# Decode attention with a gated MLP mix: K one pair ahead of V, and the weighted sum of V in four column groups

## The chip, the cores and the metric

The kernel runs on one core of a Trainium2 chip. The metric is the time of one execution on the device in microseconds (us); a kernel's figure is the median over repeated runs. A profile is taken of one further execution; its "span" reaches from the first to the last instruction.

## What is computed

Two branches get the same two rows `x` (batch B = 2, one position, D = 1024) and are mixed by a gate. Branch A is attention against a long cache: 32 heads, 16384 positions, 128 elements a head, all in bf16.

```python
# A: attention of one query row against the cache
q = (x @ wq) split in 32 heads                    # B, H, 1, 128
scores = einsum("bhqd,bhkd->bhqk", q, k_cache) * 128 ** -0.5
p = softmax(scores)
a = (einsum("bhqk,bhkd->bhqd", p, v_cache) as rows) @ wo
# B: a small MLP on the same rows
h = gelu(layernorm(x) @ w1); hs = shifted(h) @ w2; x1 = x + hs
b = x1 + gelu(layernorm(x1) @ w3) @ w4
# mix
g = sigmoid(sum(x * gate_w)); out = g * a + (1 - g) * b
```

With one position every shifted quarter of `h` is zero, so `hs` is zero. K and V of one batch row and head are 4 MB each; the 64 pairs (b, h) together are 537 MB. The weights add some 35 MB.

## The kernel before, in words

**Tiles.** A pair's K (and V) is one tile of 128 partitions; partition p holds 128 successive positions (index j) of 128 elements. All big transfers (K, V, halves of wq, blocks of B's weights) share one pool of five slots of that size (`big`, L60). Blocks of wo (256 KB, one a head) have a pool of three.

**A pair.** The loop at L487 goes over the 64 pairs, in order of heads, with both batch rows of a head one after the other. It calls, for pair i:

- `qk_stage` (L252): K lies with positions on partitions, but the scores need its elements there. VectorE transposes K in 32x32 blocks, in eight pieces (`T`, L260), each taken as 32-bit words. Four matmuls for each piece, with a sparse copy of q (`z`, built by GpSimd at L238) as the stationary operand and 512 columns of `T` as the moving one, add up all scores of the pair in one PSUM tile `S` of 128x512 (L268).
- `softmax_stage` (L276): VectorE takes the row maxima (`m`, L279), TensorE transposes them (L281), VectorE reduces them to one (`mx`, L283), TensorE spreads it over the partitions (L285), VectorE copies it out (`nb`, L287). ScalarE computes the exponentials and row sums (`Pr`, `rs`, L290), VectorE transposes the result in 32x32 blocks (`PT`, L294).
- `pv_stage` (L298): the total of the row sums by an fp32 matmul (L304) and its reciprocal (`rinv`, L306). Then the weighted sum of V, called PV below: for each of the 128 j a matmul with V[:, j, :] as the stationary operand and one column of PT as the moving one (L309), all into one column `oc`. VectorE scales it into `OT` (L316). After the second pair of a head two matmuls with the block of wo add to `wo_acc` (L322).

**Loads.** All big loads are issued by SyncE (SP) on one queue, written out by hand: at the end of pass i come V of i+2, a block of B's weights at six of the passes, a wo block at every second one, and K of i+3. Each waits until its slot is free. So the order on the queue is ..., V(i+2), K(i+3), V(i+3), K(i+4), .... The last V (pair 63) comes in four pieces of 64, 32, 16 and 16 of the j; the last wo block follows it. B's stages run two passes after their load.

**Order on the engines.** Every engine works through its own list in order. A scheduler orders the lists from the program, by priorities near its order.

Of the kernel before, what the change touches and what calls it, by code (L numbers as in the profile page):

```python
# [10 lines left out]
FP32 = mybir.dt.float32  # L11
# [12 lines left out]
def kernel(  # L24
# [15 lines left out]
    nc = tc.nc  # L40
# [30 lines left out]
    def misc_psum(shape, dtype):  # L71
        return mps.tile(shape, dtype, tag="misc", name="misc")
# [7 lines left out]
    def load_rows(src, r0, rn, name):  # L80

        N = src.shape[1]
        t = big_tile(name)
        nc.sync.dma_start(
            out=t[:, : rn * N].rearrange("p (r n) -> p r n", n=N),
            in_=src.rearrange("(p r) n -> p r n", p=P)[:, r0 : r0 + rn, :],
        )
        return t[:, : rn * N].rearrange("p (r n) -> p r n", n=N)

    kn_tiles = {}  # L90
    vn_tiles = {}
    V_SPLIT_LAST = [NJ // 2, NJ // 4, NJ // 8, NJ // 8]

    def issue_k(i):
        if i >= NPAIR:
            return
        b, h = pairs[i]
        t = big_tile("Kn")
        nc.sync.dma_start(
            out=t[:].rearrange("p (j d) -> p j d", d=Dh),  # L100
            in_=A_k_cache[b, h].rearrange("(p j) d -> p j d", p=P),
        )
        kn_tiles[i] = t

    def issue_v(i):
        if i >= NPAIR:
            return
        b, h = pairs[i]
        t = big_tile("Vn")
        tv = t[:].rearrange("p (j d) -> p j d", d=Dh)  # L110
        src = A_v_cache[b, h].rearrange("(p j) d -> p j d", p=P)
        j0 = 0
        for n in V_SPLIT_LAST if i == NPAIR - 1 else [NJ]:
            nc.sync.dma_start(out=tv[:, j0 : j0 + n, :], in_=src[:, j0 : j0 + n, :])
            j0 += n
        vn_tiles[i] = t

    wo_tiles = {}

    def load_wo(h):  # L120
        if h >= H:
            return
        t = wpool.tile([P, D], BF16, tag="woh", name="woh")
        nc.sync.dma_start(out=t[:], in_=A_wo[h * Dh : (h + 1) * Dh, :])
        wo_tiles[h] = t

    wq_half = [load_rows(A_wq, r * (KC // 2), KC // 2, f"wq{r}") for r in range(2)]

    x_pm = const.tile([P, B, KC], BF16)
    with nc.allow_non_contiguous_dma(reason="4 KB"):  # L130
# [3 lines left out]
    gw_row = rows.tile([B, D], BF16, tag="tmp_bf")  # L134
    for b in range(B):
        nc.scalar.dma_start(out=gw_row[b : b + 1, :], in_=gate_w.rearrange("(o d) -> o d", o=1))

    issue_k(0)
    issue_v(0)
    issue_k(1)  # L140


    ident_bf = const.tile([P, P], BF16)
# [24 lines left out]
    nc.vector.memset(own[:], 0.0)  # L168
    for a in range(4):
        nc.vector.memset(own[32 * a : 32 * a + 32, 4 * a : 4 * a + 4], 1.0)  # L170
    ZW = P + 8
    NZ = 3
    z_tiles = []
# [31 lines left out]
    def compute_q():  # L205
        q_f = const.tile([P, H, B], FP32)
        for half in range(2):
            qps = misc_psum([P, H, B], FP32)
            rn = KC // 2
            for h in range(H):  # L210
                for r in range(rn):
                    nc.tensor.matmul(  # L212
                        qps[:, h, :],
                        lhsT=wq_half[half][:, r, h * Dh : (h + 1) * Dh],
                        rhs=xT[:, half * rn + r, :],
                        start=(r == 0),
                        stop=(r == rn - 1),
                    )
            if half == 0:
                nc.vector.tensor_copy(out=q_f[:], in_=qps[:])  # L220
            else:
                nc.vector.tensor_tensor(out=qT[:], in0=q_f[:], in1=qps[:], op=ALU.add)
        qs_ps = misc_psum([P, 4, NPAIR], FP32)
        for v in range(4):
            nc.tensor.matmul(
                qs_ps[:, v],
                lhsT=selv[:, v].rearrange("p a w -> p (a w)"),
                rhs=qT[:].rearrange("p h b -> p (h b)"),
                start=True,
                stop=True,  # L230
            )
        nc.vector.tensor_copy(out=qsel[:], in_=qs_ps[:].rearrange("p v n -> p n v"))

    def build_z(i):
        if i >= NPAIR:
            return
        z = z_tiles[i % NZ]
        nc.gpsimd.tensor_tensor(  # L238
            out=z[:, :, 7 : 7 + P].rearrange("p v (x e) -> p v x e", e=8)[:, :, :, 0],
            in0=qsel[:, i, :].unsqueeze(2).to_broadcast([P, 4, 16]),  # L240
            in1=own[:].unsqueeze(1).to_broadcast([P, 4, 16]),
            op=ALU.mult,
        )
# [32 lines left out]
    def softmax_stage(i):  # L276
# [18 lines left out]
        PT_tiles[i] = PT  # L295
        rs_tiles[i] = rs

    def pv_stage(i):  # L298
        b, h = pairs[i]
        PT = PT_tiles.pop(i)  # L300
        rs = rs_tiles.pop(i)
        V = vn_tiles.pop(i)[:].rearrange("p (j d) -> p j d", d=Dh)
        tot_ps = misc_psum([P, 1], FP32)
        nc.tensor.matmul(tot_ps[:], lhsT=quarter_f[:], rhs=rs[:], start=True, stop=True)  # L304
        rinv = stat.tile([P, 1], FP32, name="rinv")
        nc.vector.reciprocal(out=rinv[:], in_=tot_ps[:])  # L306
        oc = ops.tile([P, 1], FP32, name="oc")
        for j in range(NJ):
            nc.tensor.matmul(  # L309
                oc[:],  # L310
                lhsT=V[:, j, :],
                rhs=PT[:, j % CJ, j // CJ : j // CJ + 1],
                start=(j == 0),
                stop=(j == NJ - 1),
            )
        nc.vector.tensor_scalar(  # L316
            out=OT[:, h, b : b + 1], in0=oc[:], scalar1=rinv[:, 0:1], scalar2=None, op0=ALU.mult
        )
        if b == B - 1:
            woh = wo_tiles.pop(h)  # L320
            for n in range(DH2):
                nc.tensor.matmul(  # L322
                    wo_acc[n][:],
                    lhsT=OT[:, h, :],
                    rhs=woh[:, n * W : (n + 1) * W],
                    start=(h == 0),
                    stop=(h == H - 1),
                )


    def layernorm_rows(src_row, dst_row_bf):
# [72 lines left out]
    h2_acc = const.tile([P, FC, B], FP32)  # L404
    h2T = const.tile([P, FC, B], BF16)
    wt = {}
    b_ps = []

    def linear_rows(w, actT, r0, rn, dst, first, last):
        for r in range(rn):  # L410
            for n in range(DH2):
                nc.tensor.matmul(  # L412
                    dst[n][:],
                    lhsT=actT[:, r0 + r, :],
                    rhs=w[:, r, n * W : (n + 1) * W],
                    start=(first and r == 0),
                    stop=(last and r == rn - 1),
                )

    def st_ln1():  # L420
        layernorm_rows(x_row[:], xn_row[:])
        rows_to_T(xn_row[:], xn1T[:])
# [23 lines left out]
    def st_lin3(half):  # L446
        linear_cols(wt.pop(f"w3{half}"), xn2T, half * (KC // 2), KC // 2, FC, h2_acc[:], half == 0)
        if half == 1:
            gelu_T(h2_acc[:], h2T[:], FC)

    def st_lin4(half):
        if half == 0:
            b_ps.extend(misc_psum([B, W], FP32) for _ in range(DH2))
        linear_rows(wt.pop(f"w4{half}"), h2T, half * (FC // 2), FC // 2, b_ps, half == 0, half == 1)
        if half == 1:
            for n in range(DH2):
                sl = slice(n * W, (n + 1) * W)
                nc.vector.tensor_tensor(out=pre_row[:, sl], in0=x1_row[:, sl], in1=b_ps[n][:], op=ALU.add)
            nc.vector.tensor_scalar(
                out=pre_row[:], in0=pre_row[:], scalar1=omg_row[:, 0:1], scalar2=None, op0=ALU.mult  # L460
            )

    def w_load(key, src, r0, rn):
        wt[key] = load_rows(src, r0, rn, "wt")


    extra = [
        (4, lambda: w_load("w1", B_w1, 0, KC), st_lin1),
        (8, lambda: w_load("w2", B_w2, 0, KC), st_lin2),
        (14, lambda: w_load("w30", B_w3, 0, KC // 2), lambda: st_lin3(0)),  # L470
        (20, lambda: w_load("w31", B_w3, KC // 2, KC // 2), lambda: st_lin3(1)),
        (28, lambda: w_load("w40", B_w4, 0, FC // 2), lambda: st_lin4(0)),
        (32, lambda: w_load("w41", B_w4, FC // 2, FC // 2), lambda: st_lin4(1)),
    ]
    ex_load = {s * NPAIR // 64: ld for s, ld, _ in extra}
    ex_run = {s * NPAIR // 64 + 2: fn for s, _, fn in extra}

    compute_q()
    compute_gate()
    load_wo(0)  # L480
    issue_v(1)
    issue_k(2)
    build_z(0)
    build_z(1)
    st_ln1()

    for i in range(NPAIR):  # L487
        build_z(i + 2)
        qk_stage(i)
        softmax_stage(i)  # L490
        pv_stage(i)
        if i in ex_run:
            ex_run[i]()
        issue_v(i + 2)
        if i in ex_load:
            ex_load[i]()
        if i % B == B - 1:
            load_wo((i + 1) // B)
        issue_k(i + 3)

    out_row = rows.tile([B, D], BF16, tag="tmp_bf")
    for n in range(DH2):
# [40 lines left out]
```

## Time and profile before

| | |
|---|---|
| time before, median of 10 runs | 1362.32 us (1361.96 to 1363.09) |
| profiled execution, time | 1363.06 us |
| profiled execution, span | 1361.1 us |
| read from HBM | 572.53 MB, 421 GB/s over the span |
| mean granted TensorE clock | 0.737 |
| instructions in the profile, all engines | 24487 |

The page has, from the top: busy time of each engine; 40 slices of the span with tenths of busy time, the granted clock of TensorE and the rate of the DMA engines; the DMA queues; the chain of work that ended last, followed back from the end; and the costliest groups of instructions with the idle time before them and what ended it. PE is TensorE's matmuls, PEld its weight loads, DVE VectorE, ACT ScalarE, POOL GpSimd, SP SyncE. "L260" is a line of the kernel. A group reads: line, engine, operation, written tile <- read tile, shapes, count, busy us, mean ns, idle us before it and its releaser. In a row of windows the first number is the length, then busy us and count of PE, PEld, DVE, ACT and POOL, then granted clock, DMA share and GB/s.

### The profile page before, as it was taken

How to read it: one execution, taken by the hardware profiler on the slowest of the kernel's cores; microseconds unless marked ns; L12 is line 12 of the kernel's file. 1: busy time of each engine (PE TensorE's matmuls, PEld its weight loads, DVE VectorE, ACT ScalarE, POOL GpSimd, SP SyncE). 2: the span in 40 equal slices, each digit the busy share in tenths (PEclk: the TensorE clock that was granted, in tenths of full speed). 3: DMA queues.
4: the chain of work that ended last, by engine and by line, in shares of the span. 5: the costliest groups of instructions: out<-in, count | busy, mean ns of one | idle time of the engine just before them, and what ended most of it. 6: DMA issues, size and time to landing. Idle time of an engine off the chain costs nothing.

```text
span 1361.1 us, 24487 instructions
## 1 busy us (share of the span) xinstructions
PE 974.6 (72%) x11196; PEld 530.1 (39%) x11260; DVE 749.0 (55%) x948; ACT 51.8 (4%) x132; POOL 33.9 (2%) x79
## 2 busy tenths in 40 slices
PE   2776777777767676777777777767767767776776
PEld 2333344344344344434434343333433334334343
DVE  2655555565636554565545456546645655654654
ACT  0000000000000000000000000000000000000000
POOL 0000000000000000000000000000000000000000
PEclk9877767687766786876777777677678667777767
DMA  9999999999999999999999999999999999999993
GB/s 401 435 423 433 433 425 430 429 429 430 428 431 429 428 429 431 430 428 429 430 429 432 427 427 432 429 429 429 427 432 430 430 427 431 430 430 428 430 424 158
DMA packets 25011, 574.11 MB, mean 422 GB/s; under 512 B 3014, under 2 KB 3014, under 8 KB 7372
## 3 DMA queue, kind: packets, MB, share of 16 engines
q1 hardware_dynamic: 24628, 572.54, 98.3%
q8 instruction: 88, 1.44, 0.4%
q14 instruction: 15, 0.12, 0.0%
q10 hardware_dynamic: 280, 0.01, 0.0%
HBM read 572.53 MB, written 0.00 MB: 421 GB/s over the span
## 4 chain that ended last, share of the span: by engine, by line
DMA 68%; PE 19%; DVE 9%; issue 3%; ACT 1%; DVEq 0%; POOL 0%; ACTq 0%
DMA Kn<-in_A_k_cache_dram 66%; PE S L268 12%; DVE T L260 6%; PE oc L309 5%; DMA x_pm<-in_A_x_dram 2%; ACT Pr L290 1%; DVE PT L294 1%; DVE m L279 1%; PE misc L285 1%; PE misc L212 1%; PE misc L412 0%; DVE mx L283 0%; PE misc L281 0%; DVE nb L287 0%; DVE x_row L437 0%
## 5 line engine op out<-in xcount | busy, mean ns | idle before, releaser
L268 PE MATMUL S<-T,z 128*128 128x512 bf16 x1984 | 595.6, 455 | 174.8 <-DVE T L260 158.7
L260 DVE STREAM_TRANSPOSE T<-Kn 128x1024 f32<-128x1024 f32 x512 | 596.3, 1217 | 132.6 <-DMA Kn<-in_A_k_cache_dram 106.7
L268 PEld LDWEIGHTS <-z 128*128 128x128 bf16 x2048 | 227.8, 111 | 544.4 <-issue 389.8
L309 PEld LDWEIGHTS <-Vn 128*128 128x128 bf16 x8192 | 233.0, 103 | 23.2 <-issue 23.2
L309 PE MATMUL oc<-PT,Vn 128*128 128x1 bf16 x8192 | 224.7, 165 | 18.9 <-DVE rinv L306 15.8
L316 DVE TENSOR_SCALAR OT<-oc,rinv 128x1 bf16<-128x1 f32 x64 | 14.1, 221 | 226.2 <-PE oc L309 226.2
L290 ACT ACTIVATE Pr<-S,nb 128x512 bf16<-128x512 f32 x64 | 44.0, 687 | 1247.9 <-DVE nb L287 1247.9
L279 DVE TENSOR_REDUCE m<-S 128x1 f32<-128x512 f32 x64 | 44.3, 692 | 74.7 <-PE S L268 74.7
L304 PE MATMUL misc<-rs,quarter_f 128*128 128x1 f32 x128 | 28.7, 293 | 71.6 <-ACT Pr L290 71.6
L294 DVE STREAM_TRANSPOSE PT<-Pr 128x512 bf16<-128x512 bf16 x64 | 45.5, 711 | 57.9 <-ACT Pr L290 57.9
L238 POOL TENSOR_TENSOR z<-qsel,own 128x64 bf16<-128x64 bf16 x64 | 30.2, 479 | 1216.1 <-PE S L268 1209.3
L304 PEld LDWEIGHTS misc<-rs,quarter_f 128*128 128x128 f32 x128 | 23.2, 227 | 77.1 <-ACT Pr L290 77.1
L281 PE MATMUL misc<-ident_f,m 128*1 128x128 f32 x64 | 17.3, 270 | 50.1 <-DVE m L279 50.1
L285 PE MATMUL misc<-mx,nscale_f 1*128 1x1 f32 x128 | 24.2, 256 | 23.7 <-DVE mx L283 23.7
L322 PE MATMUL wo_acc<-woh,OT 128*2 128x512 bf16 x64 | 32.4, 609 | 10.0 <-DVE OT L316 10.0
L281 PEld LDWEIGHTS misc<-ident_f,m 128*1 128x1 f32 x64 | 5.1, 79 | 83.0 <-DVE m L279 83.0
L285 PEld LDWEIGHTS misc<-mx,nscale_f 1*128 1x128 f32 x128 | 18.7, 182 | 35.9 <-DVE mx L283 35.9
L283 DVE TENSOR_REDUCE mx<-misc 1x1 f32<-1x128 f32 x64 | 17.8, 278 | 23.2 <-PE misc L281 23.2
L287 DVE COPY nb<-misc 128x1 f32<-128x1 f32 x64 | 10.1, 158 | 30.1 <-PE misc L285 30.1
L212 PE MATMUL misc<-xT,wq 128*128 128x2 bf16 x256 | 7.1, 165 | 25.8 <-DVE xT L180 23.2
L412 PE MATMUL misc<-wt,h2T 128*2 128x512 bf16 x56 | 18.2, 503 | 2.6 <-DMA wt<-in_B_w_dram 2.6
L385 PEld LDWEIGHTS <-wt 128*128 128x128 bf16 x288 | 18.4, 172 | 1.3 <-DMA wt<-in_B_w_dram 0.7
(60 smaller groups left out, 90.4 us busy)
## 6 DMA issues: line engine op xcount, KB each, us to landing
Kn<-in_A_k_cache_dram SPq DMA_DIRECT2D x64, 4096.0 KB, 41.5
Vn<-in_A_v_cache_dram SPq DMA_DIRECT2D x63, 4096.0 KB, 40.0
wt<-in_B_w_dram SPq DMA_DIRECT2D x4, 3584.0 KB
wq<-in_A_wq_dram SPq DMA_DIRECT2D x2, 4096.0 KB, 17.1
woh<-in_A_wo_dram SPq DMA_DIRECT2D x32, 256.0 KB, 39.9
wt<-in_B_w_dram SPq DMA_DIRECT2D x2, 2048.0 KB
Vn<-in_A_v_cache_dram SPq DMA_DIRECT2D x1, 2048.0 KB
Vn<-in_A_v_cache_dram SPq DMA_DIRECT2D x1, 1024.0 KB
```

Source lines behind the costliest of these rows:

```text
L212: nc.tensor.matmul(qps[:, h, :], lhsT=wq_half[half][:, r, h * Dh : (h + 1) * Dh], rhs=xT[:, half * rn + r, :], start=(r == 0), stop=(r == ...
L238: nc.gpsimd.tensor_tensor(out=z[:, :, 7 : 7 + P].rearrange("p v (x e) -> p v x e", e=8)[:, :, :, 0], in0=qsel[:, i, :].unsqueeze(2).to_bro ...
L260: nc.vector.transpose(out=T[:].rearrange("p w j s -> p j w s"), in_=Kw[:, m * CW : (m + 1) * CW].rearrange("p (j w e) -> p j w e", w=2, e=32),
L268: nc.tensor.matmul(S[:], lhsT=z[:, v, 7 - m : 7 - m + P], rhs=Tb[:, v // 2, :, v % 2], start=(m == 0 and v == 0), stop=(m == NM - 1 and v ...
L279: nc.vector.reduce_max(out=m[:], in_=S[:], axis=AX.X)
L281: nc.tensor.transpose(mT[:], m[:], ident_f[:])
L285: nc.tensor.matmul(nb_ps[:], lhsT=nscale_f[:], rhs=mx[:], start=True, stop=True)
L290: nc.scalar.activation(out=Pr[:], in_=S[:], func=ACTF.Exp, bias=nb[:], scale=scale, accum_out=rs[:])
L294: nc.vector.transpose(out=PT[:].rearrange("p j m -> p (j m)"), in_=Pr[:])
L304: nc.tensor.matmul(tot_ps[:], lhsT=quarter_f[:], rhs=rs[:], start=True, stop=True)
L309: nc.tensor.matmul(oc[:], lhsT=V[:, j, :], rhs=PT[:, j % CJ, j // CJ : j // CJ + 1], start=(j == 0), stop=(j == NJ - 1),)
L322: nc.tensor.matmul(wo_acc[n][:], lhsT=OT[:, h, :], rhs=woh[:, n * W : (n + 1) * W], start=(h == 0), stop=(h == H - 1),)
```

## The change

It does four things.

1. **Order.** Transfers and steps are two lists. The steps run as: scores of pair i+1, PV of pair i, wo, a stage of B, softmax of pair i+1. The transfers have the same order: K(i+1), a block of B's weights, a wo block, V(i). A transfer is issued as soon as the step that frees its slot stands in the program. The last transfers are K63, V62, V63 in four pieces, and the last wo block. The first five big ones are the halves of wq, K0, K1 and V0.
2. **PV.** For all pairs but the last, `pv_rows` has V as the moving operand. Eight rounds m; in each, four matmuls write 32 partitions each of one PSUM tile `O` (128x512): group g takes four of the j as 512 moving columns, and all four groups have the same 32 columns of PT as the stationary operand. ScalarE copies `O` out to `Os`, and four fp32 matmuls with a selection matrix `osel` pick the wanted rows and add them up into the column `oc`. The last pair keeps the form of before (`pv_cols`).
3. **wo** has a step of its own, and its load comes one pair earlier on the queue.
4. **B.** The last linear stage adds each half to the row at once instead of keeping two PSUM tiles over several passes; the blocks are loaded two passes later by number, and used in the same pass.

```diff
+    osel = const.tile([P, 4], FP32)
+    nc.vector.tensor_copy(out=osel[:], in_=ident_f[:, 0:8:2])
+    for g in range(1, 4):
+        nc.vector.tensor_tensor(
+            out=osel[:], in0=osel[:], in1=ident_f[:, 40 * g : 40 * g + 8 : 2], op=ALU.add
+        )
...
+    def pv_rows(V, PT, oc):
+        O = ops.tile([P, 4 * Dh], FP32, name="O")
+        for m in range(NM):
+            lhsT = PT[:].rearrange("p j m -> p (j m)")[:, m : CJ * 32 : 16]
+            for g in range(4):
+                j0 = m * CJ + 4 * g
+                nc.tensor.matmul(
+                    O[32 * g : 32 * g + 32, :],
+                    lhsT=lhsT,
+                    rhs=V[:, j0 : j0 + 4, :],
+                    start=(m == 0),
+                    stop=(m == NM - 1),
+                )
+        Os = rows.tile([P, 4, Dh], FP32, name="Os")
+        nc.scalar.copy(out=Os[:].rearrange("p x d -> p (x d)"), in_=O[:])
+        for x in range(4):
+            nc.tensor.matmul(
+                oc[:], lhsT=Os[:, x, :], rhs=osel[:, x : x + 1], start=(x == 0), stop=(x == 3)
+            )
...
-        oc = ops.tile([P, 1], FP32, name="oc")
-        for j in range(NJ):
...
+        oc = misc_psum([P, 1], FP32)
+        (pv_rows if i < NPAIR - 1 else pv_cols)(V, PT, oc)
...
     def st_lin4(half):
-        if half == 0:
-            b_ps.extend(misc_psum([B, W], FP32) for _ in range(DH2))
-        linear_rows(wt.pop(f"w4{half}"), h2T, half * (FC // 2), FC // 2, b_ps, half == 0, half == 1)
+        ps = [misc_psum([B, W], FP32) for _ in range(DH2)]
+        linear_rows(wt.pop(f"w4{half}"), h2T, half * (FC // 2), FC // 2, ps, True, True)
+        for n in range(DH2):
+            sl = slice(n * W, (n + 1) * W)
+            nc.vector.tensor_tensor(
+                out=pre_row[:, sl], in0=(x1_row if half == 0 else pre_row)[:, sl], in1=ps[n][:], op=ALU.add
+            )
...
-    for i in range(NPAIR):
-        build_z(i + 2)
-        qk_stage(i)
-        softmax_stage(i)
-        pv_stage(i)
-        if i in ex_run:
-            ex_run[i]()
-        issue_v(i + 2)
-        if i in ex_load:
-            ex_load[i]()
-        if i % B == B - 1:
-            load_wo((i + 1) // B)
-        issue_k(i + 3)
+    for i in range(-1, NPAIR):
+        if i + 1 < NPAIR:
+            xfers.append(("big", f"k{i + 1}", lambda i=i: load_k(i + 1)))
+            steps.append((f"k{i + 1}", lambda i=i: (build_z(i + 1), qk_stage(i + 1))))
+        if i >= 0:
+            h = i // B
+            last = h == H - 1
+            if i in extra:
+                xfers.append(("big", f"x{i}", extra[i][0]))
+            if i % B == 0 and not last:
+                xfers.append(("wo", f"o{h}", lambda h=h: load_wo(h)))
+            xfers.append(("big", f"v{i}", lambda i=i: load_v(i)))
+            if i % B == B - 1 and last:
+                xfers.append(("wo", f"o{h}", lambda h=h: load_wo(h)))
+            steps.append((f"v{i}", lambda i=i: pv_stage(i)))
+            if i % B == B - 1:
+                steps.append((f"o{h}", lambda h=h: wo_stage(h)))
+            if i in extra:
+                steps.append((f"x{i}", extra[i][1]))
+        if i + 1 < NPAIR:
+            steps.append(("", lambda i=i: softmax_stage(i + 1)))
...
+    for name, run in steps:
+        issue_ready()
+        run()
+        done.add(name)
```

`issue_ready` goes down the list of transfers and issues each whose slot, five big transfers (or three wo blocks) back, belongs to a step that is done.

More of the change, by code (lines that the diff above doesn't have):

```diff
@@ L91, with load_k @@
     vn_tiles = {}
+    wo_tiles = {}
     V_SPLIT_LAST = [NJ // 2, NJ // 4, NJ // 8, NJ // 8]
-    def issue_k(i):
-        if i >= NPAIR:
-            return
+    def load_k(i):
         b, h = pairs[i]
@@ L103, in issue_k, with load_v @@
         kn_tiles[i] = t
-    def issue_v(i):
-        if i >= NPAIR:
-            return
+    def load_v(i):
         b, h = pairs[i]
@@ L116, in issue_v @@
         vn_tiles[i] = t
-    wo_tiles = {}
     def load_wo(h):
-        if h >= H:
-            return
         t = wpool.tile([P, D], BF16, tag="woh", name="woh")
@@ L125, in load_wo @@
         wo_tiles[h] = t
-    wq_half = [load_rows(A_wq, r * (KC // 2), KC // 2, f"wq{r}") for r in range(2)]
     x_pm = const.tile([P, B, KC], BF16)
@@ L136 @@
         nc.scalar.dma_start(out=gw_row[b : b + 1, :], in_=gate_w.rearrange("(o d) -> o d", o=1))
-    issue_k(0)
-    issue_v(0)
-    issue_k(1)
     ident_bf = const.tile([P, P], BF16)
@@ L170 @@
         nc.vector.memset(own[32 * a : 32 * a + 32, 4 * a : 4 * a + 4], 1.0)
+    assert CJ == 16
+    osel = const.tile([P, 4], FP32)
[4 more added lines that the diff above has]
+        )
     ZW = P + 8
@@ L296, in softmax_stage, with pv_cols @@
         rs_tiles[i] = rs
+    def pv_rows(V, PT, oc):
[17 more added lines that the diff above has]
+            )
+    def pv_cols(V, PT, oc):
+        for j in range(NJ):
+            nc.tensor.matmul(
+                oc[:],
+                lhsT=V[:, j, :],
+                rhs=PT[:, j % CJ, j // CJ : j // CJ + 1],
+                start=(j == 0),
+                stop=(j == NJ - 1),
+            )
     def pv_stage(i):
@@ L306, in pv_stage @@
         nc.vector.reciprocal(out=rinv[:], in_=tot_ps[:])
-        oc = ops.tile([P, 1], FP32, name="oc")
-        for j in range(NJ):
[L309 to L315, printed above, removed]
+        oc = misc_psum([P, 1], FP32)
+        (pv_rows if i < NPAIR - 1 else pv_cols)(V, PT, oc)
         nc.vector.tensor_scalar(
@@ L318, in pv_stage, with wo_stage @@
         )
[L319 to L328, printed above, removed]
+    def wo_stage(h):
+        woh = wo_tiles.pop(h)
+        for n in range(DH2):
+            nc.tensor.matmul(
+                wo_acc[n][:],
+                lhsT=OT[:, h, :],
+                rhs=woh[:, n * W : (n + 1) * W],
+                start=(h == 0),
+                stop=(h == H - 1),
+            )
     def layernorm_rows(src_row, dst_row_bf):
@@ L406 @@
     wt = {}
-    b_ps = []
     def linear_rows(w, actT, r0, rn, dst, first, last):
@@ L451, in st_lin4 @@
     def st_lin4(half):
-        if half == 0:
-            b_ps.extend(misc_psum([B, W], FP32) for _ in range(DH2))
-        linear_rows(wt.pop(f"w4{half}"), h2T, half * (FC // 2), FC // 2, b_ps, half == 0, half == 1)
+        ps = [misc_psum([B, W], FP32) for _ in range(DH2)]
+        linear_rows(wt.pop(f"w4{half}"), h2T, half * (FC // 2), FC // 2, ps, True, True)
+        for n in range(DH2):
+            sl = slice(n * W, (n + 1) * W)
+            nc.vector.tensor_tensor(
+                out=pre_row[:, sl], in0=(x1_row if half == 0 else pre_row)[:, sl], in1=ps[n][:], op=ALU.add
+            )
         if half == 1:
-            for n in range(DH2):
-                sl = slice(n * W, (n + 1) * W)
-                nc.vector.tensor_tensor(out=pre_row[:, sl], in0=x1_row[:, sl], in1=b_ps[n][:], op=ALU.add)
             nc.vector.tensor_scalar(
@@ L467 @@
     extra = [
[L468 to L473, printed above, removed]
-    ]
-    ex_load = {s * NPAIR // 64: ld for s, ld, _ in extra}
@@ L476 @@
[L476 to L485, printed above, removed]
-    for i in range(NPAIR):
-        build_z(i + 2)
-        qk_stage(i)
-        softmax_stage(i)
-        pv_stage(i)
-        if i in ex_run:
-            ex_run[i]()
-        issue_v(i + 2)
-        if i in ex_load:
-            ex_load[i]()
-        if i % B == B - 1:
-            load_wo((i + 1) // B)
-        issue_k(i + 3)
+        (6, lambda: w_load("w1", B_w1, 0, KC), st_lin1),
@@ new lines @@
+        (10, lambda: w_load("w2", B_w2, 0, KC), st_lin2),
+        (16, lambda: w_load("w30", B_w3, 0, KC // 2), lambda: st_lin3(0)),
+        (22, lambda: w_load("w31", B_w3, KC // 2, KC // 2), lambda: st_lin3(1)),
+        (30, lambda: w_load("w40", B_w4, 0, FC // 2), lambda: st_lin4(0)),
+        (34, lambda: w_load("w41", B_w4, FC // 2, FC // 2), lambda: st_lin4(1)),
+    ]
+    extra = {s * NPAIR // 64: (ld, fn) for s, ld, fn in extra}
+    wq_half = []
+    xfers = []
+    steps = []
+    for r in range(2):
+        xfers.append(("big", "q", lambda r=r: wq_half.append(load_rows(A_wq, r * (KC // 2), KC // 2, f"wq{r}"))))
@@ new lines @@
+    steps.append(("q", compute_q))
+    steps.append(("gate", compute_gate))
+    steps.append(("ln1", st_ln1))
+    for i in range(-1, NPAIR):
[19 more added lines that the diff above has]
+            steps.append(("", lambda i=i: softmax_stage(i + 1)))
@@ new lines, with issue_ready @@
+    ring_size = {"big": 5, "wo": 3}
+    ring_used = {"big": [], "wo": []}
+    done = set()
+    def issue_ready():
+        while xfers:
+            ring, freed_by, load = xfers[0]
+            used = ring_used[ring]
+            if len(used) >= ring_size[ring] and used[-ring_size[ring]] not in done:
+                return
+            load()
+            used.append(freed_by)
+            xfers.pop(0)
+    for name, run in steps:
+        issue_ready()
+        run()
+        done.add(name)
@@ L501 @@
+    assert not xfers
     out_row = rows.tile([B, D], BF16, tag="tmp_bf")
```

## The prediction

> **What bounds the kernel now.** I read the DMA rows of the page first, then the groups of instructions, then the chain of waits, then the last 20 us in windows.
>
> ```profile
> PE 974.6 (72%) x11196; PEld 530.1 (39%) x11260; DVE 749.0 (55%) x948; ACT 51.8 (4%) x132; POOL 33.9 (2%) x79
> ...
> DMA  9999999999999999999999999999999999999993
> ...
> q1 hardware_dynamic: 24628, 572.54, 98.3%
> q8 instruction: 88, 1.44, 0.4%
> ```
>
> All 16 DMA engines are busy in every slice but the last: 572.54 MB at 427 to 432 GB/s. A K and a V are 8.39 MB, so a pair needs 8.39 / 429 = 19.55 us; half a wo block (0.13 MB) makes it 19.86. Unless the bytes or the rate change, time can be won only at the two ends, and lost wherever the engines need more than 19.86 us for a pair.
>
> ```profile
> L260 DVE STREAM_TRANSPOSE T<-Kn 128x1024 f32<-128x1024 f32 x512 | 596.3, 1217 | 132.6 <-DMA Kn<-in_A_k_cache_dram 106.7
> ...
> L279 DVE TENSOR_REDUCE m<-S 128x1 f32<-128x512 f32 x64 | 44.3, 692 | 74.7 <-PE S L268 74.7
> ```
>
> VectorE waits 106.7 us for K, some 1.7 us a pair: that is the slack of the engines' own chain. The end is another matter:
>
> ```profile
> 1296.50 41.72 DMA Kn<-in_A_k_cache_dram
> ...
> 1338.24 1.26 DVE T L260
> ...
> 1349.43 0.70 DVE m L279
> ...
> 1350.48 0.29 DVE mx L283
> ...
> 1352.30 0.72 DVE PT L294
> ...
> 1353.06 3.57 PE oc L309 x128
> ...
> 1356.93 0.60 PE wo_acc L322
> ...
> 1358.29 0.66 DVEq L538
> ```
>
> The last K lands at 1338.2, and everything after it (transposes and scores 11.2, softmax 3.6, PV 3.6, wo and output 4.5) stands bare: 22.9 us to the end at 1361.1. The last V comes behind that K, yet nobody waits for it. The windows show who delivers it:
>
> ```profile
> 1330.00:1332.00 2.00, 0.65 (x3) 0.37 (x3) 0.63 (x3) 0.44 (x1) 0.00 (x0) 1.00 0.85 353
> 1332.00:1334.00 2.00, 1.25 (x37) 1.18 (x38) 0.77 (x2) 0.34 (x2) 0.00 (x0) 1.00 0.55 239
> 1334.00:1344.00 10.00, 6.85 (x109) 4.13 (x108) 5.70 (x6) 0.00 (x0) 0.00 (x0) 0.51 0.52 217
> 1344.00:1346.00 2.00, 2.00 (x9) 0.79 (x8) 1.62 (x3) 0.00 (x0) 0.00 (x0) 0.87 0.48 194
> 1346.00:1348.00 2.00, 2.00 (x11) 0.84 (x10) 2.00 (x3) 0.00 (x0) 0.00 (x0) 1.00 0.40 160
> 1348.00:1350.00 2.00, 1.39 (x6) 0.35 (x4) 0.85 (x2) 0.00 (x0) 0.00 (x0) 1.00 0.01 3
> ```
>
> The last columns are granted clock, DMA share and GB/s. From 1332 to 1347 the share is a half: eight engines finished near 1331.6, eight work until 1347.6. K63 landed at 1338.2, 9.4 us before the late half was through with the V and the wo block behind it; so it is the late half that sets a landing. What that half did besides is the instruction queue: 88 packets, 1.44 MB. TensorE ran 22,456 instructions (11,196 + 11,260), and 1.44 MB over these is 64 bytes each, so this queue is TensorE's program. I take it (an inference from the half share) that the eight late engines fetch it: 11 packets each, and 16 us of lag over 11 is 1.45 us a packet.
>
> **The change, part by part.**
>
> *Order of transfers.* The last ones were V62, K63, V63, wo31; they become K63, V62, V63, wo31. The last K lands one V (9.8 us) earlier. Behind it the engines now do K63's scores (10.9), then PV of pair 62, then softmax, then PV of 63.
>
> *TensorE's program.* 63 of 64 pairs lose 128 matmuls and 128 weight loads and get 32 of each, plus 4 fp32 matmuls that run as two passes, as at L304: 256 become 80. 22,456 - 63 x 176 = 11,368 instructions, so 44.5 packets, 5.6 for each late engine. The lag falls from 16 to 8.1 us, and all late landings come 7.9 us earlier. Ends: nothing, if the lag has another cause; 7.9. I take 7.9, since count and bytes fit.
>
> *The engines' chain for a pair.* VectorE and TensorE alternate, so it is serial. On TensorE the order is scores of i+1, PV of i, the four selections, the transpose of m, wo, nb, total; on VectorE eight transposes, m, OT, mx, nb, PT, rinv.
> - Transposes and scores: (596.3 + 24.3 waiting for TensorE + 74.7) / 64 = 10.87 us.
> - PV of pair i, X, follows at once; V has landed by then (9.8 < 10.87). m (0.69) now hides under it.
> - New: ScalarE copies O. Nearest row: the exp over 128x512, 0.69, with 0.2 of handover: 0.89.
> - New: four fp32 selections, each two passes as L304 (0.30 us of loads, 0.08 more for the end): 1.28.
> - Transpose of m and handover, 0.31; mx to the end of PT, 1350.48 to 1353.02, 2.54; rinv 0.13.
> - wo stands before nb on TensorE's queue; every second pair nb waits some 0.4: 0.2 on average.
>
> Sum 16.2 + X. Queued behind the selection that now waits for ScalarE are the transpose of m, wo and nb; behind OT on VectorE are mx and the next K's transposes. So each term counts in full.
>
> *X* has no row: no matmul here targets 32 columns. Nearest is L412, 128x512 matmuls at granted clock 1.00, six to seven in 1 us, 0.216 each by the clock ratio to the 0.427 pitch at clock 0.50. PV comes right behind the scores, where windows in mid-kernel show 1.00. Floor, four groups at once: 8 x 0.216 = 1.7. Ceiling, one after another: 32 x 0.216 = 6.9. The row alone says 6.9, hence 23.1 us a pair and some 200 us lost. The Trainium skill, "TensorE: Matmul & The Clock Gate", Part 3, lists three column tiles with 512 moving columns at 2.38 times one by one: 6.9 / 2.38 = 2.9, hence 19.1 a pair, under 19.86. The same part has a rule against the change: a weight load overlaps a running matmul only if their row groups differ, and here all four groups use all rows, with a load before each matmul. Against that stands L268: loads of all 128 rows start while the matmul before is running, and its cold pitch stays at 0.43. "TensorEngine Tiling (Array Packing)", Restrictions, adds that column tiling loses the fast weight load; no run here shows by how much, and I cost it at nothing, since L268's loads of 128 columns (0.11 us) hide under a matmul. I take 2.9, with 1.7 and 6.9 kept as ends.
>
> *Depth of the buffers.* Five slots as before. V(i+2) takes K(i+1)'s slot when its transposes end, some 39 us before it must land; K(i+4) takes V(i)'s, some 45 us. Before: 40.0 and 41.5. No starving; V's release after PV costs nothing. The start has the same four big loads queued for the first 39 us, so SP's later wait of wo0 and V0 for x (22 us) is hidden. The B weights come ahead of a V instead of ahead of a K, and st_lin4 frees its banks twice, two adds of 0.67 on 2 rows: within the slack.
>
> *The end.* K63 lands at 1338.2 - 9.8 - 7.9 = 1320.5. Scores to 1331.4, PV of 62 to 1334.3, copy and selections to 1336.5, softmax to PT at 1339.3. The late half ends at 1347.6 - 7.9 = 1339.7, the last V piece some 0.7 before, so both meet. PV of 63 in the old form, 3.57: 1342.9. Then OT, wo, output as before (1356.63 to 1361.1): span 1347.4. The profiled execution took 1363.06, 1.96 around its span; the median of the runs is 0.74 below it. 1347.4 + 1.96 - 0.74 = 1348.6.
>
> **Rivals.**
> 1. *Forecast, 1348.6: chance 0.50.* Range of its own 1345 to 1353: X down to 1.7 takes 1.2 off the end; lateness carried into the last pairs adds some us.
> 2. *Only the order counts, 1356.5: 0.20.* The lag has another cause and stays. K63 at 1328.4 plus 26.9 ends the span at 1355.3. For it: eight engines as fetchers is only inferred. Against: 88 packets on eight engines at about 1 us are already some 11 of the 16 us (0.4% of 16 x 1361 = 87 us).
> 3. *The chain of a pair becomes the bound: slower, 0.27.* One place, X. It decides from X = 3.7, where 16.2 + X passes 19.86, and is slower than before from 3.8. The time is then 34 (first transpose) + 64 x (16.2 + X) + 43 (the B matmuls, 18.4 + 24.6) + 5. X = 4.5 gives 1407; X = 6.9 gives 1560. For it: no row shows overlapping column groups, and a cold clock at the selections (four times the 0.50 us of loads that L304 shows at the lower clock, 2.0 for 1.28) would eat nearly all of the 0.8 of slack. Against: 2.9 leaves those 0.8.
> 4. *It cancels, within 0.2%: 0.03.* X about 3.8: a slightly slow chain uses up the gain of the end.
>
> What a measurement here can tell from no change is 0.2%, 2.7 us. Rivals 1 and 2 make faster 0.70, rival 4 same 0.03, rival 3 slower 0.27. The range reaches from 1344 (X = 1.7, and a lag 3 us smaller than taken) up to 1385, which takes in rival 2 and the mild cases of 3; the rest of 3, under 0.2, is left out.
>
> **What would show it.** The new PV group: 32 matmuls in some 2.9 us, starts of four close together (X). VectorE still waiting for K in most pairs (chain under 19.86). The instruction queue near 45 packets, and the half-share stretch at the end about 8 us long instead of 16 (rival 2: 16 still). The last K landing near 1320, the wait before the last PV on PT or the last V piece, no longer 41 us on Kn. I am wrong if the DMA rows drop below 9 in mid-span: then rival 3 holds.

## The result and the profile after

The changed kernel takes 1348.2 us (median of 8 runs, 1347.7 to 1348.81) against 1362.32 (28 runs): ratio 0.9896, 95% interval 0.9887 to 0.9904. The forecast was 1348.6. Its profiled execution took 1348.63 us around a span of 1346.8.

Three rows of the page of the changed kernel: the engines, the DMA share in 40 slices, the instruction queue.

```profile
PE 928.6 (69%) x5652; PEld 445.9 (33%) x5716; DVE 743.8 (55%) x954; ACT 88.4 (7%) x195; POOL 34.4 (3%) x79
...
DMA  9999999999999999999999999999999999999996
...
q8 instruction: 44, 0.72, 0.2%
```

The DMA engines are still busy in every slice but the last, and that one is now busy to 6 tenths instead of 3. TensorE ran 11,368 instructions (5652 + 5716), the number of the prediction, and its queue fetched 44 packets for 88.

The groups of the page (busy us, mean ns | idle before and its releaser) that answer to the prediction's terms:

```profile
L255 DVE STREAM_TRANSPOSE T<-Kn 128x1024 f32<-128x1024 f32 x512 | 596.1, 1216 | 125.5 <-DMA Kn<-in_A_k_cache_dram 100.2
L302 PE MATMUL O<-Vn,PT 128*32 128x512 bf16 x2016 | 133.0, 409 | 41.9 <-DMA Vn<-in_A_v_cache_dram 41.8
...
L310 ACT COPY Os<-O 128x512 f32<-128x512 f32 x63 | 36.9, 585 | 1006.4 <-PE O L302 1006.4
L312 PE MATMUL misc<-osel,Os 128*128 128x1 f32 x504 | 67.1, 254 | 47.2 <-ACT Os L310 47.2
```

VectorE still waits 100.2 us for K, so the engines' chain stays under the transfers. The new PV is busy 133.0 / 63 = 2.11 us a pair, X in the prediction; the copy takes 0.585, the four selections 67.1 / 63 = 1.07.

The end of the chain of waits of the changed kernel (start us, length, what):

```profile
1274.63 46.52 DMA Kn<-in_A_k_cache_dram
...
1321.25 1.25 DVE T L255
...
1332.48 1.92 PE O L302 x32
...
1334.48 0.59 ACT Os L310
...
1335.11 1.07 PE misc L312 x8
...
1338.09 0.71 DVE PT L289
...
1338.86 3.56 PE misc L318 x128
...
1342.72 0.60 PE wo_acc L344
```

The last K lands at 1321.15 instead of 1338.2, 17.1 us earlier. What follows it has grown from 22.9 to 25.65 us, since PV of pair 62 with its copy and selections now lies between the last scores and the last softmax. 17.1 - 2.75 is the whole gain of 14.3 us in the span.

The windows of its end (last columns: granted clock, DMA share, GB/s):

```profile
1330.00:1332.00 2.00, 2.00 (x11) 0.87 (x9) 1.36 (x2) 0.00 (x0) 0.00 (x0) 1.00 0.82 340
1332.00:1338.00 6.00, 3.93 (x46) 2.35 (x43) 1.26 (x4) 1.31 (x3) 0.00 (x0) 1.00 0.55 230
1338.00:1340.00 2.00, 1.64 (x45) 1.58 (x46) 0.77 (x2) 0.06 (x1) 0.00 (x0) 0.56 0.37 142
1340.00:1346.00 6.00, 3.42 (x93) 2.40 (x89) 1.62 (x3) 0.00 (x0) 0.00 (x0) 0.50 0.02 8
```

Read as in the prediction, the early half of the DMA engines is through near 1331.5 as before; the late half ends in the row from 1338 to 1340, not at 1347.6. The stretch of half share is 8 us instead of 16.

### The profile page after: what moved, and what is told of

It is laid out like the page before. It is cut to its first block, busy times and chain, and to the rows that moved or that the text cites. A ratio compares the mean times of both kernels' runs of the same rounds, so it can differ in the third digit from the quotient of the medians.

```text
span 1346.8 us, 13464 instructions
## 1 busy us (share of the span) xinstructions
PE 928.6 (69%) x5652; PEld 445.9 (33%) x5716; DVE 743.8 (55%) x954; ACT 88.4 (7%) x195; POOL 34.4 (3%) x79
## 3 DMA queue, kind: packets, MB, share of 16 engines
q1 hardware_dynamic: 24628, 572.54, 99.2%
## 4 chain that ended last, share of the span: by engine, by line
DMA 65%; PE 24%; DVE 7%; issue 3%; ACT 1%; DVEq 0%; POOL 0%; ACTq 0%
DMA Kn<-in_A_k_cache_dram 44%; DMA Vn<-in_A_v_cache_dram 20%; PE S L263 14%; PE O L302 5%; DVE T L255 5%; DMA x_pm<-in_A_x_dram 2%; PE misc L407 1%; PE misc L433 1%; PE misc L312 1%; ACT Pr L285 1%; ACT Os L310 1%; PE misc L207 1%; DVE PT L289 0%; PE misc L280 0%; PE misc L318 0%
## 5 line engine op out<-in xcount | busy, mean ns | idle before, releaser
L255 DVE STREAM_TRANSPOSE T<-Kn 128x1024 f32<-128x1024 f32 x512 | 596.1, 1216 | 125.5 <-DMA Kn<-in_A_k_cache_dram 100.2
L263 PEld LDWEIGHTS <-z 128*128 128x128 bf16 x2048 | 238.6, 117 | 552.5 <-issue 398.4
L302 PE MATMUL O<-Vn,PT 128*32 128x512 bf16 x2016 | 133.0, 409 | 41.9 <-DMA Vn<-in_A_v_cache_dram 41.8
L337 DVE TENSOR_SCALAR OT<-misc,rinv 128x1 bf16<-128x1 f32 x64 | 14.1, 221 | 245.5 <-PE misc L312 241.9
L302 PEld LDWEIGHTS <-PT 128*32 128x32 bf16 x2016 | 70.0, 143 | 102.3 <-DMA Vn<-in_A_v_cache_dram 50.5
L310 ACT COPY Os<-O 128x512 f32<-128x512 f32 x63 | 36.9, 585 | 1006.4 <-PE O L302 1006.4
L312 PE MATMUL misc<-osel,Os 128*128 128x1 f32 x504 | 67.1, 254 | 47.2 <-ACT Os L310 47.2
L312 PEld LDWEIGHTS misc<-osel,Os 128*128 128x128 f32 x504 | 61.8, 193 | 78.3 <-ACT Os L310 78.3
L332 PE MATMUL misc<-rs,quarter_f 128*128 128x1 f32 x128 | 34.9, 342 | 67.0 <-ACT Pr L285 67.0
L332 PEld LDWEIGHTS misc<-rs,quarter_f 128*128 128x128 f32 x128 | 29.8, 288 | 72.7 <-ACT Pr L285 72.3
L344 PE MATMUL wo_acc<-woh,OT 128*2 128x512 bf16 x64 | 21.1, 414 | 6.0 <-DVE OT L337 6.0
## 6 DMA issues: line engine op xcount, KB each, us to landing
wq<-in_A_wq_dram SPq DMA_DIRECT2D x2, 4096.0 KB, 17.1
```

The source lines that it names most:

```text
L255: nc.vector.transpose(out=T[:].rearrange("p w j s -> p j w s"), in_=Kw[:, m * CW : (m + 1) * CW].rearrange("p (j w e) -> p j w e", w=2, e=32),
L263: nc.tensor.matmul(S[:], lhsT=z[:, v, 7 - m : 7 - m + P], rhs=Tb[:, v // 2, :, v % 2], start=(m == 0 and v == 0), stop=(m == NM - 1 and v ...
L302: nc.tensor.matmul(O[32 * g : 32 * g + 32, :], lhsT=lhsT, rhs=V[:, j0 : j0 + 4, :], start=(m == 0), stop=(m == NM - 1),)
L310: nc.scalar.copy(out=Os[:].rearrange("p x d -> p (x d)"), in_=O[:])
L312: nc.tensor.matmul(oc[:], lhsT=Os[:, x, :], rhs=osel[:, x : x + 1], start=(x == 0), stop=(x == 3))
```

## Experiments

The theory: of the 17.1 us by which the last K lands earlier, 9.9 come from its place in the queue and 7.2 from TensorE's shorter program, whose fetch burdens half of the DMA engines. The first four runs take these apart.

### The order alone

```diff
-        (pv_rows if i < NPAIR - 1 else pv_cols)(V, PT, oc)
+        pv_cols(V, PT, oc)
```

> The new order of transfers and steps, with the old PV (128 matmuls of one column) in all pairs. Theory (two gains: 7.0 us from the order, 7.3 from TensorE's shorter program): the instruction queue is back at 88 packets, the stretch of half DMA share at the end at 16 us; the last K lands near 1328.4 and 26.0 us follow it: span 1354.4, median 1355.7. Rival (the lag of eight DMA engines has another cause, and came down with the order of the transfers): last K near 1321, half share 8 us, 1348.5.

Measured: 1355.12 us (1354.61 to 1355.54), ratio to before 0.9945 [0.9932, 0.9959]. The queue fetched 88 packets and K63 landed at 1328.3. Two windows of this run's end, the transposes of the last K in its timeline, then two pieces of its chain:

```profile
1332.00:1338.00 6.00, 5.94 (x25) 2.36 (x24) 5.53 (x5) 0.00 (x0) 0.00 (x0) 0.97 0.54 231
...
1340.00:1346.00 6.00, 4.35 (x133) 3.99 (x130) 1.38 (x5) 0.78 (x2) 0.00 (x0) 0.72 0.49 202
```

```profile
1328.32 9.21 DVE L255 STREAM_TRANSPOSE T<-Kn 128x1024 f32<-128x1024 f32 x8 [1.22 <-DMA Kn<-in_A_k_cache_dram]
```

```profile
1304.36 43.41 DMA Vn<-in_A_v_cache_dram
1347.81 0.60 PE misc L318 x16
```

The half share lasts to 1346 again. The order alone moved the last K 9.9 us forward, and about half of the gain came with it. The expectation came close in time (1355.7), but for its path it was wrong: not the last K but the last V piece, landed at 1347.8, sets the end here, and only 16 matmuls of PV come after it.

### The new PV alone

The old order of transfers and steps, with `pv_rows` for all pairs but the last, inside the old loop:

```diff
-        oc = ops.tile([P, 1], FP32, name="oc")
...
+        oc = misc_psum([P, 1], FP32)
+        (pv_rows if i < NPAIR - 1 else pv_cols)(V, PT, oc)
```

> The old order of transfers and steps, with the new PV (four column groups) in all pairs but the last; B's last stage frees its banks as in the change. Theory: 44 packets on the instruction queue, half share 8 us, last K near 1330.9, then 22.9 us as before: span 1353.8, median 1355.2. Rival (the lag has nothing to do with PV's form): last K at 1338, 1362.3. A second rival (it is the form of PV, how V is read, and not the length of the program, that brings the lag down) says 1355 here too.

Measured: 1356.44 us (1355.03 to 1357.69), ratio 0.9954 [0.9941, 0.9966]; 45 packets, and the DMA share falls to 0.06 from 1340 on. So the DMA engines are through as early as in the changed kernel. The median lies 1.2 us over the expectation, which is within the spread of the five runs; but the path was not the expected one, for the last K did not set the end. Two groups of the profiled execution, which was the slowest of the five:

```profile
L267 DVE STREAM_TRANSPOSE T<-Kn 128x1024 f32<-128x1024 f32 x512 | 594.9, 1214 | 34.4 <-PE S L275 20.6 <-DMA Kn<-in_A_k_cache_dram 11.8
...
L314 PE MATMUL O<-Vn,PT 128*32 128x512 bf16 x2016 | 178.6, 515 | 20.2 <-DVE rinv L346 18.2 <-DVE PT L301 2.1
```

VectorE's wait for K is down to 11.8 us, and the same 32 matmuls are busy 2.83 us a pair for 2.11. In the old loop PV comes after the softmax. PV of pair 61 takes 3.64 us at a granted clock of 0.50, PV of pair 62 1.96 us at 1.00. Before both of them TensorE waited 1.06 us for the exponentials, so what set the clock there is not shown. Behind the scores, as in the change, a matmul of PV takes 409 ns on average for 515 here. In the profiled execution the new PV without the new order makes the engines' chain the bound: its chain of waits has no transfer in it from 1240 us to the end.

### The program's length alone

88, and then 44, idle matmuls with their weight loads for each pair, in front of a pair's scores; TensorE idles there until the next K is transposed.

```diff
+    def pad():
+        dps = misc_psum([P, 1], FP32)
+        for k in range(88):
+            nc.tensor.matmul(
+                dps[:], lhsT=ident_bf[:], rhs=ident_bf[:, 0:1], start=(k == 0), stop=(k == 88 - 1)
+            )
...
-            steps.append((f"k{i + 1}", lambda i=i: (build_z(i + 1), qk_stage(i + 1))))
+            steps.append((f"k{i + 1}", lambda i=i: (pad(), build_z(i + 1), qk_stage(i + 1))))
```

> The changed kernel with 88 idle matmuls of one column (and their weight loads) for each pair, put where TensorE waits for the next K; they write a PSUM column that nobody reads. Theory: TensorE's program is as long as before (some 88 packets), half share 16 us, last K near 1328.4, median 1355.5; up to 1 us more where the padding doesn't fit in the wait. Second rival (PV's form, not the program's length): last K near 1321, half share 8 us, 1348.2.

> As the run with 88, with 44 idle matmuls for each pair. Theory: 66 packets, half share 12 us, last K near 1324.8, 1351.9 (half way). Second rival: 1348.2.

Measured: 1355.71 us (1355.48 to 1356.37) with 88, 1351.82 (1351.06 to 1352.17) with 44. From the page of the run with 88, its instruction queue, and from its windows and timeline the end:

```profile
q8 instruction: 88, 1.44, 0.4%
```

```profile
1340.00:1346.00 6.00, 3.82 (x46) 2.52 (x46) 1.44 (x5) 1.36 (x3) 0.00 (x0) 1.00 0.49 207
```

```profile
1328.80 4.62 DVE L255 STREAM_TRANSPOSE T<-Kn 128x1024 f32<-128x1024 f32 x4 [0.44 <-DMA Kn<-in_A_k_cache_dram]
```

And from the run with 44:

```profile
q8 instruction: 66, 1.08, 0.3%
```

```profile
1325.29 4.62 DVE L255 STREAM_TRANSPOSE T<-Kn 128x1024 f32<-128x1024 f32 x4 [3.38 <-DMA Kn<-in_A_k_cache_dram]
```

In these two runs PV, order and V are those of the changed kernel; only idle instructions are added, and the last K's transposes start at 1321.25, 1325.29 and 1328.80 with 44, 66 and 88 packets. That is 0.17 us of landing time a packet. So it is not the form of PV that helps, but that it needs fewer instructions. With 88 the padding also eats into the chain of a pair (VectorE's wait for K falls to 32.7 us in all), so the cleaner of the two is the run with 44, where that wait is 99.2 for 100.2: 3.6 us of time for 22 packets.

That the fetch itself causes the lag, through eight engines that do all of it, stays an inference. The profile doesn't say which engine carried a packet, and packets and instructions rise together in these runs. Spread over eight engines, the slope is an estimated 1.4 us a packet, while the 88 packets of the page (0.4% of 16 engines' span) take about 1 us each. What makes up the rest is open.

### What the overlap of the groups is worth

The same 32 matmuls in another order: one group after the other, and two by two.

```diff
-        for m in range(NM):
-            lhsT = PT[:].rearrange("p j m -> p (j m)")[:, m : CJ * 32 : 16]
-            for g in range(4):
+        for g in range(4):
+            for m in range(NM):
+                lhsT = PT[:].rearrange("p j m -> p (j m)")[:, m : CJ * 32 : 16]
```

> The changed kernel with the two loops of the new PV swapped: all eight rounds of one column group, then the next group. Theory (matmuls of different groups overlap, those of one group can't): the 32 matmuls take 6.9 us for 1.95, the chain of a pair 22.5 us (17.5 in the changed kernel plus 5.0), over the 19.86 of the transfers: VectorE no longer waits for K, and by the prediction's formula 34 + 64 x 22.5 + 48 the time is some 1520. Rival (the order of the groups doesn't matter, the overlap is something else): 1348.

> As the run with one group, with two groups in turn: eight rounds of groups 0 and 1, then of 2 and 3. Theory: 16 x 0.216 = 3.5 us for PV, chain of a pair 19.1 us, still under 19.86: the transfers go on as before and only the end grows by the 1.6 us of one PV: 1349.8. Rival (the threshold lies lower than the sum says, since the six stages of B make the chain late): 1355 or more, with VectorE's waits for K nearly gone.

Measured: 1376.74 us (two runs, 1375.96 and 1377.52), ratio 1.0105 [1.0084, 1.0125], with one group at a time; 1348.61 (1348.44 to 1349.43) with two. One pair's PV in the timeline of the run with one group, and its group of transposes:

```profile
719.55 4.72 PE L302 MATMUL O<-Vn,PT 128*32 128x512 bf16 x32
```

```profile
L255 DVE STREAM_TRANSPOSE T<-Kn 128x1024 f32<-128x1024 f32 x512 | 597.7, 1215 | 41.2 <-PE S L263 40.7
```

And one PV in the run with two groups:

```profile
711.38 2.88 PE L301 MATMUL O<-Vn,PT 128*32 128x512 bf16 x32
```

With one group at a time waits for the scores take 40.7 of VectorE's 41.2 us: the chain is the bound, and the kernel is slower than before. The mechanism of the third rival exists. Its size was wrong: 4.72 us for the expected 6.9, so 1376.7 for some 1520. The starts in the trace show that more than one matmul is under way: the first few come 216 ns apart, but then others start in between (5, 210, 62, 154 ns and so on). So groups overlap even when the program has them one after the other. Whether TensorE does this by itself is open: the profile doesn't name the group of a matmul, and the scheduler that orders the engines' lists may have mixed the groups. Two by two, one PV costs 2.88 (3.05 on average) and leaves the time within half a us of the changed kernel. So what decides lies between 2.88 and 4.72. The excess of 28.5 us over 64 pairs is 0.45 a pair, which puts it near an estimated 4.3.

### Can the end come earlier

The last K, with its scores, ahead of V61; the last wo block ahead of V63.

```diff
+    ahead(xfers, 1, f"k{NPAIR - 1}", f"v{NPAIR - 3}")
+    ahead(xfers, 1, f"o{H - 1}", f"v{NPAIR - 1}")
...
+    steps.insert([x[0] for x in steps].index(f"v{NPAIR - 3}"), s62)
+    ahead(steps, 0, f"k{NPAIR - 1}", f"v{NPAIR - 3}")
```

> The changed kernel with the last K (and its scores) one more V earlier, and the last wo block ahead of the last V: K62, K63, V61, V62, wo31, V63 in four pieces. Theory: the late DMA engines still end near 1339.6, but the last softmax is through before, so the end waits for the last PV on V's pieces and on pair 62: span some 1345.3, median 1346.7. Rival (the two softmaxes and two PVs are only pushed together and the chain ends as late): 1348.2.

Measured: 1348.73 us (1348.17 to 1348.87), no gain. Two pieces of its chain:

```profile
1291.12 39.64 DMA Vn<-in_A_v_cache_dram
...
1330.80 3.62 PE O L302 x32
```

The softmax of pair 63 stood behind PV of pair 62 in TensorE's list, and that waited for V62 until 1330.8. The granted clock was 1.00 until then and 0.53 over this PV, which took 3.62 us. Next, the softmax goes ahead of it:

```diff
+    s63 = [x for x in steps if x[0] == ""][-1]
+    steps.remove(s63)
+    steps.insert([x[0] for x in steps].index(f"v{NPAIR - 2}"), s63)
```

> As the run with the last K earlier, with the softmax of pair 63 also ahead of PV of pair 62 in the program, so that on TensorE its small matmuls no longer stand behind a PV that waits for V62. Theory: PT of 63 is done near 1332, PV of 62 ends near 1336, PV of 63 runs along with its pieces and ends near 1340, some 0.5 after the last piece: span 1344.5, median 1345.9. Rival (the last V pieces and the wo block land later than I read, so that the end can't come earlier): 1348.

Measured: 1348.05 us (1347.87 to 1348.22). The chain of this run ends so:

```profile
1301.66 39.59 DMA Vn<-in_A_v_cache_dram
1341.24 0.05 issue
1341.29 0.60 PE misc L318 x16
```

Now the last V piece, which is the last transfer of all in this run, is what the end waits for. It lands at 1341.24, not at the 1339.6 at which the late engines were expected to end. The rival was right. PV of 63 ends at 1341.9 for 1342.4, a gain of 0.5 us in the span (1346.3) that the medians (1348.05 and 1348.2) can't tell from none.

A last run put the selections in bf16 on top of that (`Os` and `osel` as BF16):

> As the run with the softmax earlier, with Os and osel in bf16: the four selections are one pass each, eight instructions of TensorE fewer for each of 63 pairs (42 packets for 44). Theory: late DMA engines end 0.35 us earlier, and the selections take some 0.5 us less on the path at the end: 1345.3 to 1345.9. Rival (the selections are covered everywhere and two packets can't be seen): the time of the run before.

Measured: 1348.12 us (1347.9 to 1348.32), 42 packets. Same: the selections are covered now, and two packets are 0.3 us by the slope above. No version here beats the changed kernel by more than the measurement can tell.

## Why the prediction was right

It was right in the time and in the two parts that it named. The order alone gave 7.2 us (1362.32 to 1355.12) and the new PV alone 5.9 (to 1356.44), together 13.1 of the 14.1 measured; 88 idle matmuls a pair took 7.5 back. How the shorter program brings the late landings forward is shown only in part, and the nearness of the sum, 1348.6 to 1348.2, owes something to luck: several terms were off and their errors cancelled.

- *Order of transfers, 9.8 us for the last K:* the run with the order alone has 9.9.
- *TensorE's program, 44.5 packets and 7.9 us:* 44 packets. The transposes' start moved by 7.5 us between 88 and 44 packets. Three lengths of the program, nearly on one straight line, show that its length sets the lag. That the late half fetches it is still an inference.
- *X = 2.9:* mis-sized. It is 1.95 at the end and 2.11 on average: four matmuls start within 10 ns, and the next round follows 0.21 us later. The nearest row, L412, gave that pitch; the factor of 2.38 for three tiles was too careful for four. The rule against the change, on weight loads that share rows with a running matmul, did not bind here: from 1332.4 to 1334.4 matmuls were busy 1.97 us of the 2.00, and 32 weight loads 1.09 us beside them.
- *Copy, selections, softmax:* the sum was 16.2 without X. From the first PV matmul to rinv the last pair took 6.44 us, 4.49 without X, for the 5.15 summed (0.89 + 1.28 + 0.31 + 2.54 + 0.13). Which of the terms was too high was not taken apart, beyond the copy and selections (1.78 from the end of PV at 1334.40 to the end of the selections at 1336.18, for 2.17). On this one pair the chain has 0.7 us more room than forecast; with the run of one group at a time, rival 3 begins near X = 4.3 and not at 3.7.
- *Ceiling of X, 6.9:* too high; groups written one after the other took 4.72.
- *The end:* K63 at 1320.5 against 1321.15 measured, scores to 1331.4 against 1332.5, selections to 1336.5 against 1336.2, PT 1339.3 against 1338.8, PV 1342.9 against 1342.4, span 1347.4 against 1346.8. The scores took 0.4 more: the forecast used the mean of all pairs, 10.9, though the last pair before had already taken 11.2. PV took less. The end of the late transfers was read too early: with the last V piece as the last transfer of all it landed at 1341.24 in the run with the softmax earlier. In the changed kernel its landing is not shown; the 128 matmuls of the last PV run without a wait from 1338.86 to 1342.42, so it cost nothing there, but it bars a further gain.
- *Rival 2, only the order counts (1356.5):* with the order alone the kernel takes 1355.1, and by another path: the last V piece, not the last K, sets the end.

## What to carry to other kernels

In a kernel like this one, whose DMA engines never rest, the time to be won is at the ends: find which transfer lands last among those with a long chain behind them, and move it ahead of one whose chain is short. The program itself comes through DMA queues too: where the DMA share at the end stands at a half for long, compare the instruction queue's packets with the lag. Here fewer instructions were worth as much as a better order. Rewriting a step with idle time around it pays only if the chain stays under the transfers, so sum that chain first, and look at the granted clock where the new work will stand.

## What I had not expected of the hardware

- 44 packets, 0.72 MB out of 573 (0.13%), go with 7.5 us of 1348 (0.56%). If half of the engines fetch them and every transfer waits for its slowest engine, that fits, but no run shows it.
- Matmuls of different column groups overlap on TensorE, also when the program has the groups one after the other: 4.72 us for 32 matmuls of 512 columns written group by group, 2.88 two by two, 1.95 four by four.
- PV's 32 matmuls took 3.62 us after a wait for V62 (granted clock 0.53) and 1.95 right behind the scores (1.00), so where a step stands in the order can double its time.
- In the run with the softmax earlier the last V piece counted as landed at 1341.24, though the DMA share from 1340 to 1342 was 0.03.
